# One tile for each result bank in the second half, and a new written order of work

## The chip, the core and the metric

The kernel runs on one core of a Trainium2 chip. The core has five engines that work side by side, each in the order of its own queue: TensorE (PE: matmuls, which write PSUM), VectorE (DVE) and ScalarE (ACT), which read PSUM and SBUF, GpSimd (POOL), which reaches SBUF alone, and SyncE (SP), which here issues every DMA. They wait for one another by semaphores. The time is the device time of one execution in microseconds, the median of several.

## What is computed

Attention through a few packed queries, then two MoE layers of one expert each, all on 4608 tokens (8 batches of 576) of 512 features:

```python
p_packed = softmax(0.125 * p @ k.T) @ v        # 8 batches x 8 heads, 32 packed rows, head size 64
x   = softmax(0.125 * q @ p_packed.T) @ p_packed       # -> [4608, 512]

h   = x @ w_in                                 # first MoE, 512 -> 2048
P   = a0 + a1*h + a2*h**2 + a3*h**3
Q   = 1 + |b0|*|h| + |b1|*h**2
x2  = (P / (Q + 1e-6)) @ w_out                 # 2048 -> 512

h   = x2 @ v_in                                # second MoE
out = (h - tanh(h)) @ v_out
```

The weights come as 64-bit floats and are taken apart on the chip. Each product is made of three fp32r matmuls: both factors are split into a high and a low part, and low x low is left out.

## The kernel before

**A plan, and its order.** Every piece of work (a group of matmuls, one elementwise step, one DMA) is given to a `Plan` by `add`, with its engine (or two engines to choose from), a cost, what it needs, a due time, and what it must stand behind. `Plan.run` gives the pieces out one by one; each engine's instructions stand in its queue in that order, and a tile framework adds the semaphores, by the tiles that each instruction reads and writes. The list `ORDER` names pieces in the order in which they are to be given; a `+` says that the second of two engines takes the piece (DVE, where the choice is POOL or DVE). When the list is at its end, or its next piece isn't ready, the plan chooses by its costs, the due times (`DUE`) and a tolerance for each engine (`SLACK`). In the kernel before, the list has 3021 pieces and ends in the middle of the superblock s = 1 of the second MoE; the plan chose the last 944.

**First half** (to about 766 us). For a block of tokens n (10 of 384 or 512) and a pair p of weight slices (8), g = 8n + p. `l1` makes h of the first MoE, 2 x (384 or 512) columns, in one PSUM tile of two banks. ACT reads it in `ft` and `fu` (lines 878 and 882), DVE in `f2` and `f3` (893 and 897); `fw`, `fq` (890) and `r` make the reciprocal of Q, `b0` to `b3` (910 to 919) the quotient's high and low part, and `l2h` and `l2l` multiply them by `w_out` into the four accumulators of `ps_acc`. `fq` and `b3`, like the steps `ss`, `sn`, `sl` of the softmax and the low parts `w2` of the weights, are done by POOL or DVE. Weight pieces are loaded by `raw.j.c` into two buffers and unpacked (`d1`, `dA`, `d`, `wh`, `w2`). The attention of a half batch u runs through `sc`, `mx`, `ex`, `et`, `ta`, `av`, `y`, `bt`, `bd`; `k`, `v`, `q`, `w1`, `w1d` and `st` are DMAs, and `g` folds the packed values into the weights (`gH`, `gL`).

**Second half.** The first 1536 tokens of the second MoE go by plain products: `l3` makes h for one slice f of 128 features (16 slices, three blocks b of 512 tokens, 12 matmuls each, line 988), `th` takes the tanh (ACT, line 1003), `su` (for b > 0 the steps g11 to g22) subtracts (DVE, line 1007). Meanwhile DVE, ACT and POOL make the sums of weights that Strassen's scheme needs (`ps`, `pm`, `ph`, `pl`), and `pb`, `pd` store them. Then come superblocks s of 1024 tokens by a Strassen-Winograd scheme with seven products: `m3(s, j, i)` is product i (in the order 1, 6, 7, 5, 2, 4, 3, six matmuls each, line 1205) of the feature block j = 0 to 7, for s = 1 to 3, and `m4(s, i, f)` the second layer, for s = 0 to 3. A j of `m3` has four result banks: a (products 1, 2), b (6), c (7, 4), d (5, 3). ACT copies a (`p1`, line 1214); DVE makes `u2` = b + p1 (1216), `u3` = c + u2 (1218), `h22` = d + u3 (1220), then `h21` = c + u2 and `h12` = d + u2 (1222, 1224).

**PSUM.** There are eight banks. Four are `ps_acc`, one tile each (acc). The other four are the pool `ps_h`: two tiles of two banks each, taken in turn by `ring` (tile name h) by everything else: `sc`, `et`, `av`, `g`, `sm`, `l1`, pairs of `l3`, and in `m3` and `m4`. In `m3` an even j takes both h tiles (a, b in one, c, d in the other), an odd j the four acc tiles. The tile framework lets a tile's writer and its readers on different engines wait for one another.

Of the kernel before, what the change touches and what calls it, by code (L numbers as in the profile page):

```python
# [35 lines left out]
l2l.1 f2.3 l1.4 fq.3 w1d.1 z.3 f3.3 dA.10 d1.10 w1d.3 ft.4 d.10 l2h.2 fu.4 g.0.6 f2.4 raw.11.0 b3.2 wh.10.0 wh.10.1
f3.4 gH.0.6 av.3 r.3 gL.0.6 w2.6+ raw.11.1 k.4 y.3 fw.4 w2.7+ w1.1.0 d1.11 l2l.2 b0.3 bt.3 l1.5 raw.12.0 raw.12.1
dA.11 bd.3 b1.3 fq.4+ ft.5 fu.5 b2.3 w1d.4 d.11 r.4 f2.5 sc.4 mx.4 raw.13.0 f3.5 b3.3 dA.12 d1.12+ ex.4 l2h.3 d.12
fw.5 sm.1 et.4 raw.13.1 wh.12.0 fq.5 ta.4 si.1 z.4 wh.12.1 l1.6 sx.1 w1d.5 w2.8+ d1.13 dA.13 ft.6 w2.9+ l2l.3 k.5 b0.4
v.4 fu.6 raw.14.0 d.13 ss.1 sc.5 f2.6 raw.14.1 mx.5 f3.6 r.5 ex.5 l2h.4 av.4 b1.4 se.1 v.5 b0.5 wh.13.1 d1.14 et.5 y.4  # L40
wh.13.0 bt.4 bd.4 sz.1 dA.14 w1d.7 g.1.0 k.6 b2.4 ta.5 w2.11+ gH.1.0 b3.4+ sn.1+ w2.10 p.3 fw.6 gL.1.0 l2l.4 gH.1.1
z.5 raw.15.0 av.5 y.5 gL.1.1 bt.5 d.14 fq.6 bd.5 so.1 g.0.7 gH.0.7 sc.6 gL.0.7 sh.1 r.6 raw.15.1 l1.7 l2h.5 ft.7 mx.6
b1.5 fu.7 sl.1+ b2.5 ex.6 wh.14.0 d1.15 b3.5 dA.15 f2.7 f3.7 w2.12+ fw.7 z.6 b0.6 d.15 et.6 wh.14.1 b1.6 l1.8 w1d.6
wh.15.0 w2.13+ l2l.5 ta.6 ft.8 v.6 w1.1.2 av.6 fq.7+ fu.8 wh.15.1 w2.14 y.6 k.7 l2h.6 r.7 w2.15 f2.8 rx f3.8 bt.6 l1.9
bd.6 g.1.2 b2.6 fw.8 b0.7 b3.6+ ft.9 l2l.6 l2h.7 fq.8+ w1.1.4 fu.9 b1.7 b2.7 gH.1.2 b3.7 gL.1.2 gH.1.3 f2.9 f3.9 l2l.7
fw.9 gL.1.3 r.8 l1.10 sp.0.0 fq.9 l1.11 sp.0.1 b0.8 r.9 b1.8 st.0.0 ft.10 b2.8 b0.9 fu.10 b3.8 l2h.8 st.0.1 f2.10
f3.10 fw.10 ft.11 b1.9 f2.11 fq.10+ g.1.4 p.4 gH.1.5 b2.9 l2h.9 fu.11 q.2 gH.1.4 f3.11 gL.1.4 gL.1.5 sm.2 fw.11 w1.1.6
l2l.8 sc.7 fq.11 si.2 r.10 l1.12 sx.2 r.11 b3.9 mx.7 b0.10 l2l.9 ex.7 b1.10 ft.12 b0.11 fu.12 ss.2+ et.7 f2.12 f3.12
z.7 fw.12 v.7 ta.7 l2h.10 av.7 fq.12 l1.13 b2.10 b1.11 se.2 sz.2 y.7 b3.10+ r.12 bt.7 ft.13 b2.11 bd.7 fu.13 f2.13
f3.13 l2h.11 sn.2 k.8 g.1.6 gH.1.6 gL.1.6 l2l.10 l1.14 gH.1.7 b3.11 gL.1.7 fw.13 fq.13+ l2l.11 r.13 fu.14 b0.12 fw.14  # L50
l1.15 b1.12 b0.13 b2.12 fq.14+ ft.14 b3.12 l2h.12 fu.15 ft.15 w1.2.0 p.5 so.2 f2.14 l2l.12 f3.14 g.2.0 fw.15 gH.2.1
f2.15 b1.13 b2.13 sh.2 l2h.13 gH.2.0 r.14 fq.15+ w1.2.2 f3.15 gL.2.0 sl.2 gL.2.1 b0.14 b1.14 sc.8 mx.8 l1.16 r.15
b2.14 ft.16 b0.15 b3.13 l2h.14 f2.16 ex.8 fu.16 l1.17 l2l.13 fw.16 f3.16 b3.14+ g.2.2 b1.15 fq.16+ ft.17 b2.15 fu.17
l2l.14 f2.17 l2h.15 gH.2.2 gL.2.2 f3.17 gH.2.3 l1.18 fw.17 fq.17+ b3.15+ r.16 gL.2.3 b0.16 r.17 b1.16 ft.18 fu.18
l2l.15 sp.1.0 sp.1.1 b0.17 l1.19 w1.2.4 b1.17 l2h.16 b2.16 fw.18 b2.17 f2.18 fq.18 f3.18 g.2.4 ft.19 st.1.1 fu.19
l2h.17 f2.19 st.1.0 f3.19 r.18 gH.2.4 b3.16 gL.2.4 q.3 gH.2.5 b0.18 fw.19 fq.19+ l1.20 b1.18 gL.2.5 l2l.16 ft.20
w1.2.6 fu.20 b2.18 sm.3 r.19 f2.20 si.3 b3.17 b3.18 f3.20 sx.3 fw.20 l2h.18 l1.21 fq.20+ b0.19 g.2.6 r.20 w1.3.0 b1.19
ft.21 l2l.17 b2.19 l2h.19 ss.3+ fu.21 b0.20 b3.19+ gH.2.7 f2.21 l2h.20 gH.2.6 gL.2.6 fw.21 fq.21 f3.21 b1.20 se.3
l2l.18 r.21 l1.22 fu.22 ft.22 l2l.19 v.8 b2.20 gL.2.7 b0.21 fw.22 b3.20+ b1.21 b2.21 sz.3 fq.22+ f2.22 z.8 l1.23 f3.22
ft.23 sn.3 l2h.21 fu.23 r.22 g.3.0 so.3 w1.3.2 f2.23 fw.23 l2l.20 f3.23 gH.3.1 b3.21 gH.3.0 et.8 l2l.21 sh.3 ta.8  # L60
fq.23 gL.3.0 gL.3.1 av.8 sl.3+ l1.24 y.8 bt.8 r.23 b0.22 b1.22 ft.24 bd.8 fu.24 b2.22 b0.23 l2h.22 l1.25 fw.24 f2.24
b3.22+ ft.25 f3.24 fq.24+ g.3.2 b1.23 b2.23 b3.23 f2.25 fu.25 w1.3.4 l2h.23 gH.3.2 f3.25 fw.25 gL.3.2 gH.3.3 fq.25+
k.9 r.24 l1.26 r.25 ft.26 gL.3.3 l2l.22 fu.26 b0.24 b1.24 b2.24 l2l.23 b0.25 fw.26 v.9 sp.2.0 l1.27 f2.26 st.2.0 fq.26
f3.26 sp.2.1 b1.25 ft.27 b3.24 st.2.1 f2.27 g.3.4 gH.3.4 gL.3.4 fu.27 f3.27 l2h.24 r.26 l1.28 gH.3.5 b2.25 b0.26
gL.3.5 fw.27 sc.9 ft.28 fq.27+ q.4 b1.26 mx.9 fu.28 ex.9 f2.28 l2h.25 b2.26 f3.28 z.9 b3.25+ w1.3.6 r.27 b0.27 b1.27
fw.28 fq.28+ l2l.24 et.9 ta.9 sm.4 si.4 r.28 l2l.25 l1.29 l2h.26 sx.4 ft.29 b3.26 fu.29 ss.4+ av.9 l2l.26 f2.29 f3.29
b0.28 y.9 g.3.6 fw.29 b2.27 fq.29+ bt.9 se.4 gH.3.7 bd.9 gH.3.6 sz.4 gL.3.6 sn.4+ k.10 l2h.27 gL.3.7 b1.28 p.6 r.29
sc.10 mx.10 ex.10 w1.4.0 l1.30 ft.30 b3.27+ b2.28 fu.30 l1.31 b0.29 so.4 l2h.28 fw.30 b1.29 sh.4 f2.30 z.10 l2l.27
ft.31 f3.30 fq.30 fu.31 f2.31 g.4.0 r.30 f3.31 et.10 b3.28 gH.4.0 gH.4.1 l2h.29 sl.4+ b2.29 gL.4.0 gL.4.1 fw.31 fq.31+
ta.10 v.10 av.10 r.31 l1.32 b0.30 b1.30 b2.30 b3.29+ y.10 bt.10 bd.10 fu.32 l2l.28 l1.33 l2l.29 b0.31 fw.32 ft.32  # L70
fq.32+ f2.32 l2h.30 r.32 f3.32 ft.33 b3.30+ f2.33 fu.33 b1.31 l2l.30 k.11 b2.31 b3.31+ fw.33 w1.4.2 f3.33 fq.33+ r.33
b0.32 l1.34 g.4.2 b1.32 l2h.31 b2.32 l2l.31 ft.34 gH.4.3 gH.4.2 f2.34 gL.4.2 fu.34 f3.34 fw.34 sp.3.0 gL.4.3 w1.4.4
sp.3.1 l1.35 fq.34 b3.32+ fu.35 b0.33 g.4.4 b1.33 b2.33 ft.35 gH.4.4 l2h.32 gL.4.4 gH.4.5 f2.35 l2h.33 fw.35 st.3.1
r.34 gL.4.5 fq.35 f3.35 r.35 l1.36 b0.34 b1.34 ft.36 b0.35 b3.33+ sc.11 b1.35 fu.36 l2h.34 st.3.0 f2.36 f3.36 fw.36
# [1851 lines left out]
```

## Time and profile before

| | |
|---|---|
| median of 3 runs | 1509.12 us (1508.44 to 1509.66) |
| profiled execution | 1511.86 us, span of its instructions 1509.7 us |
| PE busy / DVE / ACT / POOL | 1449.2 / 1249.9 / 891.0 / 268.8 us |
| PE clock granted, mean | 0.988 of full speed |
| moved by DMA | 257.86 MB |
| chain that ended last | PE 79% of the span, DVE 11%, ACT 5% |

A busy time is the union of an engine's instructions. Matmuls overlap in their records and their ends are modelled, so two matmuls 0.23 us apart stand there with 0.39 us each, and a gap of PE looks shorter than it is; the distance between starts is the sounder measure. In a timeline, instructions of one line and form that follow each other closely are one row with a count; the bracket says how long the engine was idle before it, and who ended that.

### The profile page before, as it was taken

Reading aid. Unit: us, or ns where it says so; the run is one execution under the profiler, and the core shown is the slowest. Engines: PE = TensorE matmul, PEld = TensorE weight load, DVE = VectorE, ACT = ScalarE, POOL = GpSimd, SP = SyncE. Lnnn points to the kernel's source line nnn. Section 1 sums busy time; section 2 is a strip of 40 time slices with the busy share of each in tenths; the row PEclk is TensorE's granted clock in tenths of the full one; section 3 lists DMA queues with packets and bytes.
Section 4 is the critical chain, followed back from the end, with each engine's and each line's share of the span. In section 5 each row is a group of like instructions: output and inputs, shape, how many; then the busy total and the mean of one; then the engine's idle time right before and its main releaser. Section 6 shows DMA issues by size and latency. Waiting matters only on the chain.

```text
span 1509.7 us, 21786 instructions
## 1 busy us (share of the span) xinstructions
PE 1449.2 (96%) x8448; PEld 1192.3 (79%) x8448; DVE 1249.9 (83%) x1590; ACT 891.0 (59%) x1232; POOL 268.8 (18%) x167
## 2 busy tenths in 40 slices
...
GB/s 305 240 261 179 91 56 128 88 129 57 177 56 87 137 56 112 56 115 60 64 163 180 258 237 265 270 285 235 205 194 278 229 181 213 232 213 195 209 199 136
DMA packets 74998, 257.86 MB, mean 171 GB/s; under 512 B 7184, under 2 KB 25744, under 8 KB 60048
## 3 DMA queue, kind: packets, MB, share of 16 engines
...
q8 instruction: 67, 1.10, 0.3%
q14 instruction: 35, 0.29, 0.1%
...
## 4 chain that ended last, share of the span: by engine, by line
PE 79%; DVE 11%; ACT 5%; issue 2%; DMA 1%; POOL 1%; SPq 0%; DVEq 0%; ACTq 0%; POOLq 0%
PE acc L868 20%; PE acc L1205 19%; PE h L1205 15%; PE h L855 11%; PE h L988 8%; PE h L721 2%; DVE t L893 1%; DVE t L897 1%; PE acc L1028 1%; PE acc L1029 1%; PE acc L1030 1%; ACT u L882 1%; DVE gh L910 1%; DMA raw<-in_w_dram 1%; DVE m L912 1%
## 5 line engine op out<-in xcount | busy, mean ns | idle before, releaser
L855 PE MATMUL h<-ah,slot 128*128 128x320 f32 (+3 forms) x1024 | 215.1, 304 | 0.0
L868 PE MATMUL acc<-gh,slot 128*128 128x512 f32 (+1 forms) x800 | 171.8, 366 | 0.0
L855 PEld LDWEIGHTS h<-ah,slot 128*128 128x128 f32 x1024 | 170.7, 193 | 1.1
L868 PE MATMUL acc<-raw,slot 128*128 128x512 f32 (+1 forms) x720 | 165.4, 380 | 0.7 <-DVE raw L910 0.7
L868 PEld LDWEIGHTS acc<-gh,slot 128*128 128x128 f32 x800 | 143.5, 188 | 25.9 <-issue 8.9
L855 PE MATMUL h<-al,slot 128*128 128x192 f32 (+3 forms) x512 | 151.0, 308 | 9.8 <-DVE t L897 5.1
L868 PEld LDWEIGHTS acc<-raw,slot 128*128 128x128 f32 x720 | 130.3, 188 | 33.0 <-issue 8.7
L1244 ACT ACTIVATE yh<-slot 128x512 fp32r<-128x512 f32 x140 | 87.7, 631 | 73.6 <-DVE yl L1248 25.5
L855 PEld LDWEIGHTS h<-al,slot 128*128 128x128 f32 x512 | 98.4, 192 | 19.5 <-issue 7.7
L1248 DVE TENSOR_TENSOR yl<-slot,yh 128x512 fp32r<-128x512 f32 x140 | 98.3, 714 | 17.8 <-ACT yh L1244 17.3
L878 ACT ACTIVATE t<-h,coa 128x1024 f32<-128x1024 f32 (+1 forms) x80 | 89.2, 1117 | 39.1 <-PE h L855 39.0
L893 DVE TENSOR_TENSOR t<-t,h 128x1024 f32<-128x1024 f32 (+1 forms) x80 | 88.5, 1110 | 26.7 <-ACT u L882 26.1
L882 ACT ACTIVATE u<-h 128x1024 f32<-128x1024 f32 (+1 forms) x80 | 74.8, 935 | 46.5 <-PE h L855 13.8
L897 DVE SCALAR_TENSOR_TENSOR t<-t,coa,h 128x1024 f32<-128x1024 f32 (+1 forms) x80 | 93.6, 1171 | 6.0 <-ACT u L882 4.4
L868 PE MATMUL acc<-gl,slot 128*128 128x384 f32 (+1 forms) x400 | 93.9, 378 | 2.6 <-POOL gl L919 1.3
L988 PE MATMUL h<-xh,slot 128*128 128x512 f32 x256 | 84.0, 402 | 3.6 <-DVE slot L1007 2.8
L868 PEld LDWEIGHTS acc<-gl,slot 128*128 128x128 f32 x400 | 73.9, 195 | 16.2 <-issue 3.1
L1205 PE MATMUL h<-slot,rg 128*128 128x512 f32 x336 | 80.8, 393 | 5.3 <-DVE slot L1220 2.3
L1244 ACT ACTIVATE yh<-ex 128x512 fp32r<-128x512 f32 x84 | 53.1, 632 | 51.3 <-PE acc L1205 16.9
L1205 PEld LDWEIGHTS h<-slot,rg 128*128 128x128 f32 x336 | 62.2, 188 | 22.6 <-DVE slot L1220 5.2
L1205 PE MATMUL acc<-yh,raw 128*128 128x512 f32 x256 | 78.9, 389 | 0.0
L1205 PE MATMUL acc<-yh,rg 128*128 128x512 f32 x256 | 78.8, 389 | 0.0
...
## 6 DMA issues: line engine op xcount, KB each, us to landing
...
```

Of the source, the lines that this page charges most:

```text
L721: pe.matmul(out=ps[32 * hp:32 * hp + 32, i, :], lhsT=pp[b][r, hp, :], rhs=x[r, hp, :])
L855: pe.matmul(out=ps[:, f, t], lhsT=x, rhs=y, start=(i == 0), stop=(i == len(seq) - 1))
L868: pe.matmul(out=acc_t[n][m][:, 0:XW[n]], lhsT=w2_slot[2 * p + f][:, o:o + 128], rhs=x[:, f, :], start=(p == 0 and part == 512 and f == 0), ...
L878: act.activation(out=t_t[g], in_=hv(g), func=AF.Identity, scale=a3, bias=a2)
L882: act.activation(out=u_t[g], in_=hv(g), func=AF.Abs)
L893: dve.tensor_tensor(out=t_t[g], in0=t_t[g], in1=hv(g), op=ALU.mult)
L897: dve.scalar_tensor_tensor(out=t, in0=t, scalar=a1, in1=hv(g), op0=ALU.add, op1=ALU.mult)
L910: dve.scalar_tensor_tensor(out=gh_t[g], in0=t, scalar=a0, in1=r, op0=ALU.add, op1=ALU.mult)
L988: pe.matmul(out=hy(b, f), lhsT=a, rhs=w, start=(j == 0), stop=(j == len(seq) - 1))
L1205: pe.matmul(out=to, lhsT=a, rhs=b, start=(first and n == 0 and i in (1, 6, 7, 5)), stop=(last and n == len(seq) - 1), skip_group_check=True,)
L1244: act.activation(out=yh_t[s, i, f], in_=g_of(GSRC[i], f), func=AF.Copy)
L1248: by.tensor_tensor(out=yl_t[s, i, f], in0=g_of(GSRC[i], f), in1=yh_t[s, i, f].bitcast(F32), op=ALU.subtract)
```

## The change

1. `ps_h` is closed after the first half (`open banks`, ordered behind the last `f3`), and its four banks come back as four tiles of one bank each. `pair` hands them out two by two, in the turn that `ring` would have had next. `l3`, `m3` and `m4` use `pair`.
2. The plan learns that readers of one PSUM tile on different engines come one after the other: `add` takes `on`, `run` remembers when each engine has last read that tile, and `apart` puts a start behind the other engines' reads. It is given for `gH`, `gL`, `ft`, `fu`, `f2`, `f3`.
3. The plan's latency of a load goes from 3.0 to 4.0 us for `k`, `v`, `q`, `p`, `w1`, `w1d`, `id` and the first 16 `raw`; `DUE` and `SLACK` have new numbers.
4. Three pieces get an order among themselves: `xr` of the first block behind its first, `th.3` behind `th.2`, `l3.0` behind the new `open b` in place of the last `l1`.
5. `ORDER` is new from the first line on, and names all 3965 pieces.

```diff
-SLACK = {"ALT": 0, "DVE": 0.0, "PE": 468.9, "ACT": 81.3, "POOL": 0.0, "SP": 0.0}
+SLACK = {"ALT": 0, "DVE": 7.5, "PE": 525.8, "ACT": 0, "POOL": 0, "SP": 734.4}
...
 ORDER = """
...
-wh.6.1 fw.1 w2.3+ q.1 fq.1+ dA.7 l1.2 gL.0.4 d1.7 b2.0 d.7 b3.0 av.2 ft.2 fu.2 y.2 raw.8.0 f2.2 raw.8.1 bt.2 f3.2
-g.0.5 r.1 b0.1 bd.2 d1.8+ raw.9.0 dA.8 v.3 l2l.0 raw.9.1 fw.2 d.8 gH.0.5 fq.2+ wh.8.1 wh.8.0 gL.0.5 sc.3 mx.3 w2.5
...
+d1.6+ dA.6 ft.1 b0.0 d.6 v.2 gH.0.3 gL.0.3 wh.6.1 l2h.0 av.2 w2.3+ fu.1 f2.1 wh.6.0 raw.7.1 w2.2 fw.1 f3.1 y.2 dA.7
+b1.0 fq.1+ k.3 p.2 g.0.4 gH.0.4 b2.0 b3.0 bt.2 bd.2 w1d.2 w1d.3 raw.8.0 gL.0.4 sc.3 l1.2 d1.7 mx.3 r.1 ex.3 raw.8.1
+d.7 ft.2 b0.1 fu.2 w1.1.0 b1.1 d1.8+ dA.8 d.8 fw.2 f2.2 et.3 l2l.0 fq.2 raw.9.0 ta.3 f3.2 wh.8.0 l2h.1 w2.4+ raw.9.1
...
+        seen = {}
+
+        def apart(engine, x):
+
+            return max([t for e, t in seen.get(x[10], {}).items() if e != engine], default=0)
...
-            return t
+            return max(t, apart(engine, x)) if x[10] else t
...
+            if x[10]:
+                seen.setdefault(x[10], {})[engine] = end[name]
...
-    ps_h = pool_of(ctx, "ps_h", bufs=2, space=PSUM)
+    sh = ctx.enter_context(ExitStack())
+    ps_h = pool_of(sh, "ps_h", bufs=2, space=PSUM)
+    banks_p, uses = [], []
...
     def ring(key):
+        uses.append(key)
         ps_t[key] = ps_h.tile([128, 2, 512], F32, tag="h", name="h")
         return ps_t[key]
+
+    def open_banks():
+        sh.close()
+        banks_p.append(pool_of(ctx, "ps_b", space=PSUM))
+
+    def pair(key):
+        i = len(uses) % 2
+        uses.append(key)
+        ps_t[key] = [banks_p[0].tile([128, 512], F32, tag=f"b{i}{x}", name=f"b{i}{x}") for x in range(2)]
+        return ps_t[key]
...
     def hy(b, f):
-        return ps_t[f // 2, "y", b][:, f % 2, :]
+        return ps_t[f // 2, "y", b][f % 2]
...
-                t = ring(("m3", s, j, 0))
-                bank["a"], bank["b"] = t[:, 0, :], t[:, 1, :]
+                bank["a"], bank["b"] = pair(("m3", s, j, 0))
...
-            t = ring(("m4", s, i))
+            t = pair(("m4", s, i))
...
+    add(("open b",), None, 0, open_banks, [], 0, behind=[("f3", total - 1)])
...
-            kw["behind"] = [("l1", total - 1)]
+            kw["behind"] = [("open b",)]
```

## Rows read from the trace of the kernel before

**Rows 1.** The page, busy time, share of the span and instructions of each engine.

```profile
PE 1449.2 (96%) x8448; PEld 1192.3 (79%) x8448; DVE 1249.9 (83%) x1590; ACT 891.0 (59%) x1232; POOL 268.8 (18%) x167
```

**Rows 2.** Stretches: length; busy PE, PEld, DVE, ACT, POOL; clock; DMA share; GB/s.

```profile
0.00:50.00 50.00, 25.13 (x255) 15.47 (x255) 26.38 (x42) 25.59 (x42) 1.85 (x8) 0.84 0.80 272
50.00:100.00 50.00, 41.36 (x367) 33.62 (x366) 46.13 (x58) 46.36 (x64) 12.13 (x8) 0.92 0.85 287
100.00:150.00 50.00, 46.24 (x437) 39.09 (x438) 43.56 (x53) 42.35 (x62) 15.87 (x9) 0.97 0.51 176
150.00:766.00 616.00, 606.87 (x4211) 509.09 (x4210) 572.29 (x585) 439.91 (x522) 156.64 (x74) 1.00 0.25 93
766.00:1037.00 271.00, 266.72 (x1166) 218.00 (x1165) 219.32 (x319) 140.85 (x218) 54.57 (x49) 0.99 0.70 242
1037.00:1114.00 77.00, 72.31 (x312) 57.55 (x311) 40.36 (x61) 23.40 (x42) 23.73 (x19) 1.00 0.60 206
```

**Rows 3.** Timeline of PE, s = 1: start, length, instruction, count, idle before.

```profile
1037.35 8.32 PE L1205 MATMUL h<-slot,rg 128*128 128x512 f32 x36
1047.95 9.70 PE L1205 MATMUL acc<-slot,raw 128*128 128x512 f32 x42
1057.49 1.52 PE L1205 MATMUL h<-slot,rg 128*128 128x512 f32 x6
...
1068.91 9.68 PE L1205 MATMUL acc<-slot,raw 128*128 128x512 f32 x42
1078.43 8.32 PE L1205 MATMUL h<-slot,rg 128*128 128x512 f32 x36
...
1098.57 1.52 PE L1205 MATMUL h<-slot,rg 128*128 128x512 f32 x6
...
1110.81 4.47 PE L1205 MATMUL acc<-slot,raw 128*128 128x512 f32 x19
```

**Rows 4.** Timeline of PE, s = 2 and s = 3.

```profile
1216.34 10.13 PE L1205 MATMUL h<-slot,raw 128*128 128x512 f32 x42
1226.31 9.68 PE L1205 MATMUL acc<-slot,rg 128*128 128x512 f32 x42
...
1410.20 10.14 PE L1205 MATMUL h<-slot,rg 128*128 128x512 f32 x42
1420.18 9.68 PE L1205 MATMUL acc<-slot,raw 128*128 128x512 f32 x42
```

**Rows 5.** Timeline of DVE, s = 2: `u3` on h, on acc.

```profile
1202.44 0.69 DVE L1218 TENSOR_TENSOR u<-h,u 128x512 f32<-128x512 f32 x1 [1.40 <-PE h L1205]
...
1211.55 0.69 DVE L1218 TENSOR_TENSOR u<-acc,u 128x512 f32<-128x512 f32 x1
```

**Rows 6.** Waits of PE from 766 to 1037 us: total, times, longest.

```profile
PE h L988 <- DVE slot L1007: 2.8, 2, 1.9
PE h L988 <- ACT t L1003: 1.4, 2, 0.7
```

**Rows 7.** Line 988 (`l3`): ns min/median/max, first and last start in us.

```profile
L988 PE MATMUL h<-xh,slot x256: 388/395/628, 767.0 to 960.9; 128*128 128x512 f32 x128
...
L988 PEldq EVENT_SEMAPHORE  x2: 51/51/51, 765.6 to 776.0; - x2
```

**Rows 8.** Groups of `fq` before 150 us: count, busy us, mean ns, idle before.

```profile
L890 POOL TENSOR_TENSOR m<-u,r 128x768 f32<-128x768 f32 x3 | 5.5, 1842 | 14.8 <-ACT r L886 8.3 <-DVE raw L567 4.7 <-ACT y L698 1.8
...
L890 DVE TENSOR_TENSOR m<-u,r 128x768 f32<-128x768 f32 x5 | 4.8, 952 | 0.0
```

**Rows 9.** Timeline of POOL and DVE around 639 us.

```profile
638.91 2.39 POOL L919 TENSOR_TENSOR gl<-m,r 128x1024 fp32r<-128x1024 f32 x1 [2.90 <-DVE m L890]
...
639.28 3.11 DVE L910 SCALAR_TENSOR_TENSOR raw<-t,coa,raw 128x1024 fp32r<-128x1024 f32 x1
```

**Rows 10.** Stretches of 10 us (columns as in the second group).

```profile
30.00:40.00 10.00, 4.94 (x63) 1.76 (x56) 9.04 (x16) 8.05 (x15) 1.48 (x1) 0.53 0.89 297
40.00:50.00 10.00, 7.58 (x28) 6.66 (x26) 6.60 (x9) 6.46 (x9) 0.00 (x0) 0.67 0.48 171
```

More of the change, by code (lines that the diff above doesn't have):

```diff
@@ L36 @@
[L36 to L74, printed above, removed]
-mx.11 l1.37 v.11 ex.11 b2.34 q.5 fq.36+ ft.37 l2l.32 b2.35 et.11 fu.37 w1.4.6 l2l.33 f2.37 f3.37 b3.34 ta.11 r.36
@@ new lines @@
+wh.8.1 w2.5+ l1.3 z.3 q.1 g.0.5 r.2 d1.9 b2.1 b0.2 ft.3 fu.3 dA.9 b3.1+ fw.3 raw.10.0 b1.2 f2.3 gH.0.5 d.9 f3.3
+raw.10.1 fq.3 l2l.1 gL.0.5 d1.10 b2.2 l1.4 b3.2+ v.3 av.3 dA.10 k.4 d.10 raw.11.0 fu.4 ft.4 f2.4 y.3 wh.10.1 wh.10.0
+l2h.2 fw.4 bt.3 bd.3 f3.4 w2.7+ r.3 w2.6+ sc.4 raw.11.1 sm.1 dA.11 mx.4 p.3 w1d.5 si.1 l2l.2 fq.4 ex.4 b0.3 raw.12.0
+d1.11 b1.3 r.4 d.11 b2.3 et.4 l1.5 ta.4 fu.5 raw.12.1 k.5 ft.5 dA.12 b3.3 z.4 sx.1 f2.5 g.0.6 v.4 f3.5 gH.0.6 d1.12
+ss.1 l2h.3 raw.13.0 gL.0.6 b0.4 fw.5 raw.13.1 d.12 sc.5 se.1 av.4 y.4 bt.4 w1d.7 wh.12.0 bd.4 mx.5 ex.5 l2l.3 wh.12.1
@@ new lines @@
+w2.8+ et.5 w1d.6 v.5 b1.4 fq.5+ l1.6 dA.13 w2.9+ sz.1 d1.13 ta.5 fu.6 b2.4 g.1.0 ft.6 gH.1.0 d.13 f2.6 gH.1.1 wh.13.0
+wh.13.1 raw.14.0 gL.1.0 r.5 f3.6 z.5 b3.4 l2h.4 fw.6 g.0.7 gL.1.1 gH.0.7 av.5 w2.11 raw.14.1 w2.10+ sn.1+ fq.6 gL.0.7
+so.1 y.5 dA.14 d1.14 bt.5 b0.5 d.14 k.6 l2l.4 w1d.4 v.6 bd.5 sh.1 b1.5 r.6 b2.5 sl.1 sc.6 l1.7 fu.7 ft.7 l2h.5 mx.6
+wh.14.0 f2.7 f3.7 raw.15.0 raw.15.1 ex.6 b3.5+ w2.12+ et.6 d1.15 wh.14.1 l1.8 b0.6 dA.15 d.15 w1.1.2 w2.13+ fw.7 ta.6
+ft.8 z.6 l2l.5 av.6 wh.15.0 wh.15.1 p.4 l2h.6 f2.8 fq.7 fu.8 y.6 w2.15+ w2.14 r.7 rx f3.8 b1.6 bt.6 fw.8 b0.7 b2.6
@@ new lines @@
+l2l.61 g.7.2 b1.63 f3.65 fw.65 gH.7.3 fq.65 gH.7.2 gL.7.2 r.65 l2h.63 gL.7.3 b2.63 b3.63 w1.7.4 r.64 l1.66 b0.65 fu.66
+fw.66 b0.64 b1.64 l2l.62 ft.66 b2.64 f2.66 l2l.63 b3.64 sp.7.0 sp.7.1 l1.67 l2h.64 f3.66 ft.67 fq.66+ fu.67 b1.65
+fw.67 g.7.4 l2l.64 st.7.0 st.7.1 gH.7.5 gH.7.4 l2h.65 b2.65 fq.67+ b3.65+ gL.7.4 f2.67 r.67 l2l.65 r.66 raw.16.0 q.9
+f3.67 w1.7.6 gL.7.5 b0.66 b1.66 b0.67 raw.16.1 l1.68 sm.9 b2.66 b1.67 fu.68 si.9 ft.68 b3.66 sx.9 f2.68 f3.68 fw.68
+ss.9 fq.68+ l2h.66 b2.67 l2l.66 b3.67+ d1.16 l1.69 se.9 r.68 sz.9 l2h.67 sn.9 fu.69 g.7.6 ft.69 fw.69 f2.69 dA.16
@@ new lines @@
+f3.69 so.9 gH.7.6 gL.7.6 fq.69 b0.68 b1.68 l2l.67 sh.9 gH.7.7 gL.7.7 r.69 l1.70 d.16 ft.70 fu.70 b2.68 b3.68 l2h.68
+fw.70 l1.71 f2.70 f3.70 b0.69 b1.69 fq.70+ raw.17.0 sl.9+ b2.69 l2l.68 l2h.69 b3.69 wh.16.1 fu.71 ft.71 raw.17.1 r.70
+l1.72 f2.71 open_x f3.71 fw.71 b0.70 fq.71+ l2l.69 b1.70 fu.72 l2h.70 ft.72 b2.70 l1.73 w3.1+ r.71 b3.70+ l2l.70
+xr.0.0 xr.0.1 b0.71 b1.71 fw.72 fq.72+ b2.71 d1.17 l2h.71 wh.16.0 ft.73 fu.73 f2.72 xh.0.1 r.72 b3.71 xh.0.0 f3.72
+w3.0 dA.17 fw.73 raw.18.0 l2l.71 f2.73 f3.73 l1.74 b0.72 fq.73+ sp.8.0 b1.72 sp.8.1 d.17 b2.72 xl.0.1+ r.73 b3.72+
@@ new lines @@
+l2h.72 ft.74 l1.75 b0.73 raw.18.1 fu.74 fw.74 b1.73 ft.75 fq.74+ b2.73 f2.74 st.8.1 f3.74 l2l.72 b3.73 l2h.73 xl.0.0+
+l1.76 fu.75 r.74 b0.74 fw.75 l2l.73 f2.75 f3.75 fq.75 b1.74 ft.76 l2h.74 st.8.0 xr.0.2 r.75 fu.76 l1.77 b2.74 b3.74+
+xr.0.3 b0.75 b1.75 fw.76 d1.18 fq.76+ dA.18 l2l.74 r.76 fu.77 l2h.75 xh.0.2 b2.75 b3.75 f2.76 l2l.75 fw.77 f3.76 d.18
+b0.76 wh.17.1 wh.17.0 l1.78 ft.77 wh.18.1 wh.18.0 fq.77+ w3.2+ w4.0+ xl.0.2 raw.19.0 raw.19.1 r.77 l2h.76 f2.77 f3.77
+w4.1+ ft.78 xh.0.3 w3.3+ b1.76 l1.79 fu.78 b0.77 b2.76 b3.76 ft.79 dA.19 l2h.77 f2.78 raw.20.0 xl.0.3 f3.78 d1.19
@@ new lines @@
+l2l.76 f2.79 b1.77 raw.20.1 fw.78 d.19 fq.78+ b2.77 d1.20 wh.19.0 wh.19.1 w3.4+ w4.2+ fu.79 b3.77+ dA.20 r.78 f3.79
+raw.21.0 open_b d.20 fw.79 fq.79+ l3.0.0 b0.78 l3.0.1 wh.20.0 wh.20.1 th.1 r.79 w4.3+ w3.5+ b1.78 th.0 l2l.77 l3.0.2
+raw.21.1 l2h.78 su.1 b2.78 d1.21 dA.21 th.2 raw.22.0 l3.0.3 b0.79 su.0 d.21 wh.21.1 b3.78+ wh.21.0 th.3 raw.22.1 w3.6+
+w4.4+ raw.23.0 dA.22 b1.79 d1.22 b2.79 raw.23.1 d.22 l3.0.4 wh.22.1 l2l.78 wh.22.0 l2h.79 b3.79+ w3.7+ l2l.79 dA.23
+w4.5+ sp.9.0 d1.23+ su.2 raw.24.0 l3.0.5 sp.9.1 su.3 raw.24.1 st.9.1 l3.0.6 st.9.0 open_y th.5 yh.0 d.23 yl.0 l3.0.7
@@ L232, in __init__, with add @@
         self.rings, self.work, self.aliases = dict(rings), {}, {}
-    def add(self, name, engine, cost, run, after=(), due=0.0, take=None, free=(), behind=(), late=None, port=None):
+    def add(self, name, engine, cost, run, after=(), due=0.0, take=None, free=(), behind=(), late=None, port=None, on=None):
         assert name not in self.work, name
         port = "POOL" in engine if port is None and engine else port
-        self.work[name] = [engine, cost, run, list(after), due, take, list(free), list(behind), late, port]
+        self.work[name] = [engine, cost, run, list(after), due, take, list(free), list(behind), late, port, on]
     @contextmanager
```

388 lines of the change are left out of this document (235 added, 153 removed).

## The prediction

> **What bounds the kernel now.** I read the busy line of the page first, then stretches of the run by engine, then what TensorE (PE) waited for in each stretch, and last the timeline of PE and VectorE (DVE) around those waits. PE is busy 1449.2 us of the span [rows 1], so the most that any order of work could give back is some 60 us. The stretches [rows 2] tell where those lie: 24.9 us in the first 50 (loads, before and around the first matmuls), 8.6 and 3.8 in the next two 50s, 9.1 in the 616 us of the first MoE, 4.3 in the stretch of `l3`, 4.7 in the first Strassen superblock (s = 1); what is left, some 5, comes after it. From 50 to 150 us DVE and ScalarE (ACT) are as busy as PE or busier (46 of 50), and the DMA engines are at 0.85; from 150 to 766 DVE is at 93% beside a PE at 98.5%. So the first half has three near-full engines and little to win by order alone. From 766 on PE alone is full, and each of its gaps is time lost.
>
> A busy PE row has modelled ends, so the gaps are best taken from start to start. In s = 1 the j's of `m3` (42 matmuls each) alternate: the even j's write the ring tiles (h), the odd ones the four `ps_acc` tiles. The first two odd j's last 9.54 and 9.52 us, the even ones 10.60, 11.42 and, the last, 12.24; the third even j and its odd neighbour last 20.14 together, as the first two do, so that one is 10.60 again [rows 3]. In s = 2 and 3 the row of an even j is 10.13 us long, that of an odd one 9.68 [rows 4], where the first unbroken pair and the last stand for eight even j's alike. Nothing differs between them but the tile: an h tile is one tile of two banks. [rows 5] shows what that does: on h, step `u3` (reads bank c) starts 1.40 us late, released by PE, which was still writing the other bank of that tile; on acc, `u3` follows its predecessor directly and runs beside PE's writes to another bank.
>
> **The change, part by part.**
>
> *Banks of m3.* The pairs become two tiles each, so that an even j has the odd j's situation. s = 1: 10.60 + 11.42 + 10.60 + 12.24 - 4 x 9.53 = 6.7 us. s = 2 and 3: 8 x 0.45 = 3.6 us. Together 10.3 us, all on PE's path, because PE does nothing else in that time. The ends: 10.3, if every even j becomes an odd one; 3.6, if the extra 0.6 to 2.3 us of the s = 1 ones belong to DVE's order of work there and come back. DVE is only 40.4 of 77 us busy in that stretch [rows 2], so I take 10.3. What is late next is DVE's own queue: `h22` stands behind `u3`, and `m3` of i = 3 waits for it, with a slack of two groups of six matmuls.
>
> *Banks of l3.* PE waits 2.8 us for DVE and 1.4 for ACT in this stretch [rows 6], in four pieces, where `th` and `su` of a pair ran late and PE came back to the tile. With single banks the next `l3` needs only the `su` of its own bank. But here DVE is 219 of 271 us busy [rows 2] with the making of Strassen weights, whose order is new too. Ends: 4.2 gained, or 2 lost if the new order puts more of that work ahead of a `su`; I take half, 2.1.
>
> *More tiles, more waits.* 24 pairs of `l3`, 24 of `m3` and 8 of `m4` may each need one wait more on PE's sequencer, at 51 ns [rows 7]: 56 x 0.051 = 2.9 us at most. They lie ahead of matmuls that are queued already, so I take nothing; if that cover goes, it is the 2.9.
>
> *open b, and the `behind` of l3.0, xr and th.3.* The old pool closes when `f3` of the last group has been given, so `l3.0` is ordered behind it. PE has `l2h`, `l2l` work of the last groups in both orders at that point, and both orders put two `l3` there before it ends. Nothing; at worst PE waits for one more piece of DVE, about 1 us [rows 8].
>
> *on, apart, DUE, SLACK, late.* They change what the planner believes, not what an instruction does. The new ORDER names all 3965 pieces of work (the old one 3021; the last 944 were picked by costs and due times), so these numbers pick nothing. Zero.
>
> *ORDER before 766 us.* Instructions are the same; engines of some change. Counting the marks in both orders over the first MoE, GpSimd (POOL) gets 7 more `fq` and 2 more `ss`, and 3 `b3`, 2 `sl`, 2 `w2` and 1 `sn` less: one piece more of some 86. In the opening, POOL has six `fq` instead of four up to `b3.8`. Such an `fq` takes 1.84 us there and 0.95 on DVE [rows 8], so two chains to `l2h` grow by 0.9. On SP's queue the last weight piece of the first MoE (`raw.15.1`) stands behind 1.1 MB more than before, `raw.11.1` behind 1.6 MB (the load `w1.1.0` and the stores `w1d` come earlier); `raw.7.1` stands behind 0.65 MB less. At 287 GB/s [rows 2] that is 3.9 and 5.7 us later, 2.3 earlier. Against that, `av.2` and `bt.2`, which stood back to back and left PE waiting for ACT, now have `g.0.4` between them. Signs on both sides: zero, with ends of 10.8 gained (half of the 8.6 + 3.8 + 9.1 us of idle PE) and 7.5 lost (5.7 + 2 x 0.9).
>
> A POOL piece is not free for DVE: while POOL ran a `b3` of 2.39 us, a DVE instruction that began 0.37 us after it took 3.11 and ended 1.09 us after it: some 2.0 us of standing [rows 9]. The Trainium skill ("SBUF — State Buffer", section "Who interferes with whom") says that a VectorE instruction with two SBUF inputs is shut out for the whole of a GpSimd instruction that reads SBUF. By that rule each of the seven moved `fq` could cost DVE 2.0 us of standing where it saves one piece of 0.95, up to 7 us in all; by the count of pieces above, one more on POOL in 86, it is 1.
>
> The sum: 10.3 + 2.1 = 12.4 us. The profiled execution took 1511.86 us (span 1509.7 and 2.2 around it), 2.7 above the median of the runs shown, 1509.12. So 1499.5 beside the profiled execution, 1496.7 beside the median: I forecast **1496.7**.
>
> **The rivals.**
>
> *The opening pays it back (slower).* Place: 60 to 120 us. The loads of `raw.11` to `raw.15` come 5.7 us later, the two `fq` chains add 1.8, and PE stands for those 7.5 us. Between 30 and 50 us PE was busy 12.5 of 20 us and its granted clock was 0.53 and 0.67 [rows 10]; such a spell at a mean of 0.60, between the two levels of 1.2 and 2.4 GHz, loses another 8. Together 15.5: 1509.1 - 12.4 + 15.5 = 1512.2. It decides from the point at which the second half starts 12.4 us later. For it: three full engines leave no room to catch up. Against: the raw loads are paced by two buffers that DVE sets free, not by the DMA alone, whose share falls to 0.51 after 100 us.
>
> *The opening and the first MoE gain as well.* The plan now knows that `ft`, `fu`, `f2`, `f3` can't read h side by side, and places DVE's work accordingly. Half the idle of PE from 50 to 766 us goes: 1496.7 - 10.8 = 1485.9. Against: DVE has 93% of that stretch, so what is filled in one place is missing in another.
>
> *Only the small waits go.* The s = 1 and `l3` waits are DVE's queue, and the new order queues it as badly; 3.6 us remain: 1505.5.
>
> *It does not do what it says.* The tile tracker already keeps banks apart, and the even j's are late for another reason; 1509. [rows 5] speaks against it.
>
> **How the numbers follow.** 0.2% is 3 us, about what can be told from no change. Forecast (1490 to 1503): 0.45. Gain in the first half too: 0.15. Only the small waits: 0.17, about half of it within 3 us of before. Opening pays back: 0.17. No effect: 0.06. So faster 0.69, same 0.14, slower 0.17. The range 1484 to 1511 leaves out little at the bottom, most of the slower case at the top.
>
> **What would show it.** Even and odd j's of `m3` of 9.5 us alike, in all of s = 1 to 3: the first term right. `u3` on the new banks starting without a wait for PE: the mechanism right. No wait of `l3` above 0.7 us: the second term. The start of the first `l3` (767.0 before [rows 7]) tells the first half apart: within 3 us of that it was zero; after 775 the opening paid back; before 760 it gained. Even j's still at 10 us or more, or `l3` starting over 10 us later, make the prediction wrong.

## The result, and the profile after

The changed kernel takes **1484.01 us** (median of 4 runs, 1483.25 to 1485.63), the kernel before 1508.78: a ratio of 0.984, 95% interval 0.9823 to 0.9857. It is 24.8 us faster, twice the 12.4 forecast. A second set of 4 runs gave 1484.32 (0.9839, 0.9822 to 0.9856).

The two profiled executions have spans of 1509.72 and 1482.17 us. Cut at the first matmul of each stage, the 27.55 us between them come from here (some 3 of them lie in the execution: the profiled one of the kernel before took 1511.86 us, that much above its median):

| stretch | before | after | difference |
|---|---|---|---|
| start to `l1` of group 11 | 144.57 | 139.97 | -4.60 |
| from there to `l1` of group 79 | 616.21 | 603.09 | -13.12 |
| from there to the first `m4` | 200.40 | 201.95 | +1.55 |
| `m3`, s = 1 | 82.99 | 76.16 | -6.83 |
| `m3`, s = 2 and 3 | 156.01 | 152.33 | -3.68 |
| the four `m4`, and the end | 309.54 | 308.67 | -0.87 |

So there are two gains (17.7 in the first half, 10.5 in `m3`) and a loss between them. The changed kernel's page, and its stretches (columns as in [rows 2]):

```profile
PE 1436.9 (97%) x8448; PEld 1191.6 (80%) x8448; DVE 1237.0 (83%) x1588; ACT 897.5 (61%) x1235; POOL 280.5 (19%) x168
```

```profile
0.00:50.00 50.00, 25.57 (x257) 15.69 (x258) 27.75 (x42) 26.22 (x42) 2.20 (x8) 0.80 0.88 289
50.00:100.00 50.00, 42.28 (x426) 34.52 (x425) 46.20 (x60) 46.07 (x68) 12.41 (x7) 0.93 0.83 285
100.00:150.00 50.00, 47.70 (x412) 39.60 (x414) 47.38 (x56) 45.39 (x63) 14.82 (x8) 1.00 0.49 165
150.00:740.00 590.00, 590.00 (x4132) 496.38 (x4129) 556.00 (x570) 432.00 (x508) 155.04 (x71) 1.00 0.27 95
750.00:757.00 7.00, 0.56 (x5) 0.27 (x3) 7.00 (x9) 6.96 (x10) 0.09 (x1) 0.72 0.11 37
757.00:760.00 3.00, 3.00 (x7) 2.42 (x8) 3.00 (x4) 2.71 (x4) 0.00 (x0) 0.51 0.72 268
760.00:765.00 5.00, 5.00 (x24) 4.20 (x24) 2.02 (x4) 1.42 (x3) 0.00 (x0) 1.00 0.58 201
757.00:1021.00 264.00, 264.00 (x1159) 218.01 (x1160) 208.56 (x322) 137.09 (x211) 43.28 (x35) 0.99 0.72 242
1021.00:1098.00 77.00, 77.00 (x341) 63.75 (x341) 48.61 (x77) 26.63 (x47) 16.92 (x14) 1.00 0.62 220
```

Against [rows 2]: from 150 to 740 us PE has no idle time left in the records, and none in `l3` or `m3`. The kernel before had in the same 590 us:

```profile
150.00:740.00 590.00, 581.60 (x4066) 484.15 (x4065) 546.50 (x556) 417.78 (x495) 149.10 (x70) 1.00 0.26 95
```

One stall is new, from 750 to 757 us: PE busy 0.56 of 7 us, DVE and ACT full.

**`m3`.** PE's timeline of s = 1 after, the answer to [rows 3]:

```profile
1021.26 9.68 PE L1296 MATMUL b<-slot,rg 128*128 128x512 f32 x42
1030.79 9.68 PE L1296 MATMUL acc<-slot,raw 128*128 128x512 f32 x42
...
1078.38 9.68 PE L1296 MATMUL b<-slot,rg 128*128 128x512 f32 x42
1087.90 9.68 PE L1296 MATMUL acc<-slot,raw 128*128 128x512 f32 x42
```

Even j's (on the new banks, b) and odd ones (acc) are 9.52 us alike. `u3` on either kind, the answer to [rows 5], with 0.6 us in both places, where h had 1.40 and acc none:

```profile
1177.88 0.69 DVE L1309 TENSOR_TENSOR u<-b,u 128x512 f32<-128x512 f32 x1 [0.61 <-PE b L1296]
...
1187.40 0.69 DVE L1309 TENSOR_TENSOR u<-acc,u 128x512 f32<-128x512 f32 x1 [0.60 <-PE acc L1296]
```

**The stall.** PE's waits after 745 us (the answer to [rows 6]), and its timeline there:

```profile
PE b L1081 <- DVE t L990: 6.4, 1, 6.4
PE acc L961 <- DVE gh L1003: 0.6, 1, 0.6
```

```profile
745.93 3.08 PE L961 MATMUL acc<-gh,slot 128*128 128x384 f32 x16 [0.62 <-DVE gh L1003]
748.89 1.66 PE L961 MATMUL acc<-gl,slot 128*128 128x384 f32 x8
756.99 0.76 PE L1081 MATMUL b<-xh,slot 128*128 128x512 f32 x1 [6.44 <-DVE t L990]
757.55 0.63 PE L1081 MATMUL b<-xl,slot 128*128 128x512 f32 x1
757.98 0.63 PE L1081 MATMUL b<-xh,slot 128*128 128x512 f32 x1
```

The first `l3` waits for `f3` (line 990) of group 79, the last of all, which DVE begins only here:

```profile
755.84 1.00 DVE L990 SCALAR_TENSOR_TENSOR t<-t,coa,h 128x768 f32<-128x768 f32 x1
```

So the first pair must share banks with the last `l1`, although `pair` was meant to go on in `ring`'s turn. Which banks these are is told by the program's addresses and by no profile: the last `l1` has its h tile in banks 4 and 5, and the first pair gets banks 4 and 5 again, since the reopened pool gives out banks in the order in which its tiles are first made, whatever `pair` counts. The other two banks, which `f3` of group 78 had set free at 748.72, lay idle. Experiment 3 puts this to the test.

**The first half.** What PE waited for from 150 us on, before (up to 766, the four longest of nine), then after (up to 750, all there is):

```profile
PE h L855 <- DVE t L897: 3.7, 4, 1.9
PE acc L868 <- POOL gl L919: 1.3, 2, 0.7
PE h L721 <- PE h L855: 0.9, 1, 0.9
PE h L721 <- PE h L644: 0.8, 1, 0.8
```

```profile
PE acc L961 <- DVE gh L1003: 0.6, 1, 0.6
```

And what DVE waited for at `f2` and `f3` (lines 893 and 897; 986 and 990 after) from 0 us on, before and after:

```profile
DVE t L893 <- ACT u L882: 26.1, 21, 3.1
...
DVE t L897 <- ACT u L882: 4.4, 6, 1.1
```

```profile
DVE t L986 <- ACT t L971: 10.2, 13, 2.0
DVE t L986 <- ACT u L975: 4.5, 7, 1.4
```

Before, `f2` stood 26.1 us for `fu`, though it needs nothing that `fu` makes: both read one h tile, and the semaphores let the readers through one by one. The Trainium skill ("PSUM — Partial Sum Buffer", section "PSUM bank collisions raise a hardware error") says why readers are kept apart: two engines may not touch one bank in the same cycle, two readers included, so accesses are to be guarded bank by bank. The 26.1 us of waits agree as to readers, but they are those of the framework's semaphores; no run here shows what an unguarded access would do. The two-bank h tile guards more than that rule asks.

### The profile page after: what moved, and what is told of

It is laid out like the page before. It is cut to its first block, busy times and chain, and to the rows that moved or that the text cites. A ratio compares the mean times of both kernels' runs of the same rounds, so it can differ in the third digit from the quotient of the medians.

```text
span 1482.2 us, 21855 instructions
## 1 busy us (share of the span) xinstructions
PE 1436.9 (97%) x8448; PEld 1191.6 (80%) x8448; DVE 1237.0 (83%) x1588; ACT 897.5 (61%) x1235; POOL 280.5 (19%) x168
## 4 chain that ended last, share of the span: by engine, by line
PE 90%; DVE 4%; ACT 3%; issue 1%; DMA 1%; SPq 0%; DVEq 0%; ACTq 0%
PE acc L961 24%; PE acc L1296 19%; PE b L1296 17%; PE h L948 13%; PE b L1081 9%; PE h L801 3%; PE acc L1121 1%; PE acc L1122 1%; PE acc L1123 1%; PE h L724 1%; PE h L769 1%; DMA raw<-in_w_dram 1%; DVE t L986 1%; PE h L754 1%; DVE m L1009 0%
## 5 line engine op out<-in xcount | busy, mean ns | idle before, releaser
L961 PEld LDWEIGHTS acc<-gh,slot 128*128 128x128 f32 x800 | 143.5, 188 | 30.7 <-issue 10.7
L986 DVE TENSOR_TENSOR t<-t,h 128x1024 f32<-128x1024 f32 (+1 forms) x80 | 88.5, 1108 | 15.2 <-ACT t L971 10.2
L983 POOL TENSOR_TENSOR m<-u,r 128x1024 f32<-128x1024 f32 (+1 forms) x27 | 58.4, 2162 | 166.3 <-DVE t L986 46.6
L1081 PE MATMUL b<-xh,slot 128*128 128x512 f32 x256 | 83.3, 399 | 6.4 <-DVE t L990 6.4
L1296 PE MATMUL b<-slot,rg 128*128 128x512 f32 x336 | 77.5, 389 | 0.0
```

The costliest lines, as they stand in the source:

```text
L961: pe.matmul(out=acc_t[n][m][:, 0:XW[n]], lhsT=w2_slot[2 * p + f][:, o:o + 128], rhs=x[:, f, :], start=(p == 0 and part == 512 and f == 0), ...
L983: by.tensor_tensor(out=q_m[g], in0=u_t.pop(g), in1=r_t[g], op=ALU.mult)
L986: dve.tensor_tensor(out=t_t[g], in0=t_t[g], in1=hv(g), op=ALU.mult)
L1081: pe.matmul(out=hy(b, f), lhsT=a, rhs=w, start=(j == 0), stop=(j == len(seq) - 1))
L1296: pe.matmul(out=to, lhsT=a, rhs=b, start=(first and n == 0 and i in (1, 6, 7, 5)), stop=(last and n == len(seq) - 1), skip_group_check=True,)
```

## The experiments

Line numbers differ from kernel to kernel; `l1`, `l3` and so on are named in the text. Intervals are 95% intervals of the ratio to the kernel before, which took 1508.1 to 1508.9 us beside these runs.

**1. The banks alone.** The old order on the new tiles.

```diff
 ORDER: as before, its last 944 pieces written out as the plan chose them
-... l3.0.0 l3.0.1 ... f3.79 ...
+... f3.79 open_b l3.0.0 l3.0.1 ...
```

> The order of work, DUE, SLACK and the load latency of the kernel before, written out to the last piece, with the change's single-bank tiles for l3, m3 and m4; only l3.0.0 and l3.0.1 stand behind f3.79, where the pool closes. Theory (the tiles give the second half, the order the first): the even j's of m3 fall to 9.5 us, some 10.5 us gained there as in the changed kernel (82.99 to 76.16 us in s = 1, 1.8 in s = 2 and 3 each); the first l3 starts within 5 us of 767, late by the wait for the last f3; l3 gains the 4 us of PE's waits. So 1495 to 1500 us, and what the order is worth is the other 11 to 16. Rival (the tiles are worth only the 3.6 us of the regular even j's, the rest is the order's): m3 of s = 1 stays above 80 us, l3 at 194, 1505 us.

Measured: **1496.9 us** (0.9922, 0.9909 to 0.9936). `m3` takes 76.16 us in s = 1, 2 and 3, as in the changed kernel: 10.5 us from the tiles alone. From `l1` of group 79 to the first `m4` it takes 198.64 us (200.40 before): all that PE waits for there is at the place where the two `l3` were moved away, in PE's timeline:

```profile
762.16 2.94 PE L888 MATMUL acc<-gh,slot 128*128 128x384 f32 x16
769.12 4.61 PE L888 MATMUL acc<-gh,slot 128*128 128x384 f32 x16 [4.02 <-DVE gh L930]
773.57 1.57 PE L888 MATMUL acc<-gl,slot 128*128 128x384 f32 x8
774.98 0.39 PE L1008 MATMUL b<-xh,slot 128*128 128x512 f32 x1
```

The theory holds for `m3` and for the total. The stretch of `l3` gained 1.8 us, not the 4 expected, and the first `l3` came at 774.98, 8 us late instead of 5.

**2. The order alone.** The new order on the old tiles.

```diff
-                bank["a"], bank["b"] = pair(("m3", s, j, 0))
+                t = ring(("m3", s, j, 0))
+                bank["a"], bank["b"] = t[:, 0, :], t[:, 1, :]
```
(and so for c and d, `l3` and `m4`; no pool is closed)

> The changed kernel's whole order of work, with the old tiles of two banks kept for l3, m3 and m4 (no pool is closed). Theory (tiles second half, order first half): the first l3 starts at 749 to 752 us, since PE no longer stands 6.4 us there for the last f3; m3 goes back to 78 us in s = 2 and 3 and to 78 or more in s = 1 (7 to 10.5 us lost in all); l3 loses 2 to 6. So 1487 to 1493 us. Rival (the order would have repaired the second half without new tiles): m3 of s = 1 at 76 to 77 us, and the whole at 1481 or less.

Measured: **1519.43 us** (1.0064, 1.0047 to 1.0081): slower than the kernel before, and outside both expectations. The first half is that of the changed kernel (`l1` of group 79 at 743.05), the first `l3` starts at 750.37. Then that gain is lost and more: 11.1 us more than in the changed kernel up to the first `m4`, 1.8 in that, and in `m3` 12.95, 6.92 and 1.91. PE's waits in `m3`, s = 1, and the first j's:

```profile
PE h L1297 <- DVE u L1310: 4.1, 2, 2.0
PE h L1297 <- DVE slot L1312: 1.6, 3, 0.8
PE h L1297 <- ACT p L1306: 1.4, 2, 0.7
```

```profile
1034.18 6.96 PE L1297 MATMUL h<-slot,rg 128*128 128x512 f32 x30
1043.17 1.72 PE L1297 MATMUL h<-slot,rg 128*128 128x512 f32 x6 [2.04 <-DVE u L1310]
1045.68 2.93 PE L1297 MATMUL h<-slot,rg 128*128 128x512 f32 x6 [0.78 <-DVE slot L1312]
1048.41 11.13 PE L1297 MATMUL acc<-slot,raw 128*128 128x512 f32 x42
```

PE waits for `u3` (line 1310) to have read one bank of h before it may write the other. On pairs the new order is worse than the old one (`m3` of s = 1 takes 89.11 us, 82.99 before); on single banks both give 76.16. Banks alone -12, order alone +10.6, both -24.8: the parts don't add.

**3. The other turn of the pairs.**

```diff
     def open_banks():
         sh.close()
         banks_p.append(pool_of(ctx, "ps_b", space=PSUM))
+        for x in range(2):
+            banks_p[0].tile([128, 512], F32, tag=f"b0{x}", name=f"b0{x}")
...
-        i = len(uses) % 2
+        i = (len(uses) + 1) % 2
```

> The changed kernel, with its pairs of single banks handed out in the other turn and made in that order when the pool opens: the first l3 then writes the two banks that the last but one l1 had, which f3.78 sets free, not those of the last l1, which f3.79 sets free. Theory (the 6.4 us in which PE stands before the first l3 come from that turn alone): the gap goes, the first l3 starts 5 to 6.5 us earlier, and all after it moves along: 1477.5 to 1479.5 us. Rival (the gap is work of DVE that PE needs soon in any case, and only moves to the next l3 or l2 pieces): under 2 us gained, 1482 to 1484.

Measured: **1480.43 us** (1478.22 to 1480.87; 0.9807, 0.9794 to 0.982), 3.6 to 3.9 less than the two medians of the changed kernel, and the fastest of all. In PE's timeline the first `l3` (line 1083) now follows without a gap:

```profile
747.25 3.07 PE L963 MATMUL acc<-gh,slot 128*128 128x384 f32 x16 [0.63 <-DVE gh L1005]
750.21 1.68 PE L963 MATMUL acc<-gl,slot 128*128 128x384 f32 x8
751.73 0.39 PE L1083 MATMUL b<-xh,slot 128*128 128x512 f32 x1
```

It starts 5.4 us ahead of the last `f3`, which it had to wait for before:

```profile
757.15 1.00 DVE L992 SCALAR_TENSOR_TENSOR t<-t,coa,h 128x768 f32<-128x768 f32 x1
```

From `l1` of group 79 to the first `m4` it takes 197.63 us, 4.3 less than the changed kernel, not 6.4: 1.8 us of new waits for DVE's `su` steps come in behind it, among others. The theory holds as to the cause; the size lies between it and the rival.

**4. The engines exchanged, both ways.** 82 pieces of the first half (33 `fq`, 29 `b3`, 20 others) are done by another engine in the changed order. First the new order with the old engines, then the old order (on the new banks) with the new engines.

```diff
-... fq.0 ... b3.2+ ...
+... fq.0+ ... b3.2 ...
```

> The changed kernel, its order untouched, but 82 pieces (fq, b3, ss, sn, sl, w2, d1) of the first half go back to the engine that did them in the kernel before; GpSimd gets 7 fq less, 3 b3, 2 sl and 2 w2 more. Theory A (the first half gained by the sequence in which DVE and ACT take their pieces, so that f2 waits less for fu): little is lost, within 5 us of 1484, though the pieces were not placed for these engines. Theory B (it gained by which engine does what: DVE, the fullest beside PE, was relieved): 8 to 16 us lost, 1492 to 1500 us, PE again standing for f3 at l1.

> The banks alone (order of the kernel before, 1496.9 us), with the engines that the changed kernel gives to the 82 pieces fq, b3, ss, sn, sl, w2, d1 of the first half. Theory (an order and its engines fit only each other, as the 34 us lost by the opposite exchange say): 10 us or more slower than the banks alone, over 1507. Rival (these engines relieve DVE and carry the gain of the first half): 1480 to 1490 us.

Measured: **1518.05 us** (1.0064, 1.005 to 1.0079), 34 us lost, and **1542.16 us** (1.0226, 1.0209 to 1.0243), 45 us lost against the banks alone. In the first, theory A is refuted and B's size too small; in the second the theory holds. PE waits for `f3` at `l1` again, from 100 and from 150 us on:

```profile
PE h L875 <- DVE t L917: 7.8, 8, 3.2
```

```profile
PE h L875 <- DVE t L917: 10.2, 6, 3.0
```

These waits are only a part of the 34 and 45 us; where the rest lies is not shown. An order and its choice of engines fit only each other. How much of the 17.7 us either has by itself can't be told from these two.

**5. Openings exchanged.** The old opening (403 pieces, to `l1` of group 11) with the new rest, then the new opening (412 pieces) with the old rest; both on the new banks.

```diff
-ORDER = new[:412] + new[412:]
+ORDER = old[:403] + [pieces of new that are left]
```

> The changed kernel, but its first 403 pieces are those of the kernel before, in that order and on those engines (to l1 of group 11); from there on the pieces that are left come in the changed order. Group 11 starts at 144.6 us in the kernel before, at 140.0 in the changed one. Theory (the opening is worth those 4.6 us, the other 13 of the first half are gained between 150 and 740 us, where PE stops waiting): 1487 to 1491 us. Rival 1 (the first MoE is DVE's, so a late opening is caught up or a good one runs out): 1482 to 1486. Rival 2 (the order after 150 us only fits its own opening): over 1495.

> The other way round: the first 412 pieces (to l1 of group 11) as in the changed kernel, the rest in the order and on the engines of the kernel before, with the banks (alone they took 1496.9 us). Theory (each stretch keeps what it has: the changed opening is worth 2.5 to 4.6 us, the rest of the first MoE the other 12): l1 of group 79 at 754 to 757 us instead of 758.7, PE again waiting for f3 between 150 and 740 us, 1492 to 1495 us. Rival (the changed opening only helps because of what follows it): 1496 us or more.

Measured: **1482.35 us** (0.982, 0.9802 to 0.9838), which fits rival 1 by its time, but not by its trace. `l1` of group 11 starts at 142.61, 2.6 us after that of the changed kernel, and of group 79 at 745.90, 2.8 after: nothing is caught up. It is won back because the 7.3 us to the first `l3` hold no stall: it starts at 753.20, and the last `f3` only at 758.66. By the program's addresses the exchange shifted the h tiles by one turn: the last `l1` lies in banks 6 and 7, and the first `l3` finds 4 and 5 free, as in experiment 3. A delay at group 11 arrives whole at group 79 (in experiment 3 too: 1.3 us at both), and PE has next to no idle time between them: from 140 us on PE is the bound under the new order.

The other: **1499.46 us** (0.9939, 0.9925 to 0.9954); the rival holds. Group 11 starts at 138.50, 4.7 before that of the banks alone, group 15 at 185.35 and group 79 at 758.76 (banks alone 184.91 and 758.70). Two idle times of PE, of 1.50 and 2.09 us, take up most of it within 20 us; the rows name no releaser for them. So under the old order something other than PE sets the pace there, and a better opening is worth nothing.

**6. `f2` moved out of `fu`'s way.** In 12 groups, on the banks alone.

```diff
-... fu.7 sl.1+ b2.5 ... f2.7 f3.7 w2.12+ ...
+... fu.7 sl.1+ b2.5 ... w2.12+ f2.7 f3.7 ...
```

> The banks alone (order of the kernel before, 1496.9 us), with one thing moved: in 12 groups of the first MoE in which f2 stood at the head of DVE's queue waiting for ACT's fu on the same h tile (15.6 us of idle DVE in all), the next other DVE piece of the list goes ahead of f2 (and of f3 where it stood between). Theory (what the plan now knows of readers of one tile is what the first half gained by): the idle DVE is filled, l1 of group 79 starts 5 to 10 us sooner than 758.7, 1487 to 1492 us. Rival (f3 comes later in these groups, and PE waits for it at l1 instead, or the idle DVE is off the path): 1494 to 1502 us.

Measured: **1502.75 us** (0.9957, 0.994 to 0.9973), 5.9 slower than the banks alone; slower as the rival says, and just past its 1502. (The profiled execution, 1505.59, was the slowest of five.) DVE's wait of `f2` for `fu` fell from 17.9 to 10.7 us between 150 and 766 us, and `l1` of group 79 came 8.4 us later. In the trace PE stands twice at `l1` (groups 8 and 20) for an `f3` that the edit had put off; `z`, named in the first row, is the piece right behind that `f3`:

```profile
124.88 0.33 PE L875 MATMUL h<-al,slot 128*128 128x192 f32 x1 [2.64 <-DVE z L674]
241.55 0.48 PE L875 MATMUL h<-al,slot 128*128 128x256 f32 x1 [2.14 <-DVE t L917]
```

Both times the piece that went ahead was not ready itself, and DVE stood for it in place of `f2`:

```profile
121.96 0.86 DVE L1466 TENSOR_TENSOR slot<-raw,slot 128x512 fp32r<-128x512 f32 x1 [1.68 <-ACT slot L1462]
238.27 0.69 DVE L740 TENSOR_TENSOR slot<-h,slot 128x512 fp32r<-128x512 f32 x1 [3.89 <-ACT slot L736]
```

So the idle time was not filled but moved: between group 11 and group 79 DVE does 571.8 us of work in 615.5 on the banks alone, and 571.7 in 618.7 here. In these two places PE pays for a later `f3`; what a real filling of DVE's wait would be worth is not shown.

**7. The plan left to itself.** The new list is cut after `l1` of group 11; with what the plan knows of readers, and without.

```diff
-            return max(t, apart(engine, x)) if x[10] else t
+            return t
```

> The changed kernel with its list cut after l1 of group 11 (412 pieces): the plan chooses the other 3553 by its costs, DUE, SLACK and what it knows of the readers of one tile. All theories: slower than the changed kernel by more than 10 us, since the list was the better order; l1 of group 79 after 755 us. It is there to be set beside the next one.

> As the one before, but the plan no longer puts a reader behind the other engine's reader of the same tile (apart gives nothing). Theory (that knowledge is what keeps DVE from standing at f2): DVE waits 10 us or more longer for ACT's fu at f2, and l1 of group 79 starts 5 to 20 us later than with it. Rival (the knowledge changes the order, not the time): the two within 4 us of each other at that point.

Measured: **1522.32 us** with (1.009, 1.0069 to 1.0111), **1542.1 us** without (1.0222, 1.0203 to 1.024). `l1` of group 79 starts at 768.82 and 785.92, so the knowledge is worth 17.1 us where the plan chooses with these costs and due times (others were not tried, and they may have been set for a plan that has it). It isn't worth it by the way expected: `f2`'s wait for `fu` is not among DVE's longer waits in either. PE's waits for `f3` differ, first with, then without:

```profile
PE h L713 <- DVE t L755: 9.1, 5, 3.3
```

```profile
PE h L713 <- DVE t L755: 13.6, 8, 3.4
```

That is 4.5 of the 17.1; waits for `b0` (0.9 against 4.0 us) and `b3` (1.8 against 3.9) grow too. GpSimd's part differs as well, 46 instructions and 101.2 us after 150 us with, 38 and 82.9 without; that this is the cause isn't shown. The written list beats the better of the two by 38 us.

The changed kernel again, beside experiments 4 (second) to 6:

> The changed kernel once more, for the comparison with the others of this group on one chip: 1483 to 1486 us by every theory; its first l3 at 757 us, PE standing 6.4 us before it.

Measured: 1484.32 us, the first `l3` at 757.41, behind 6.42 us of standing PE.

## Why the prediction was right and wrong

- *Banks of m3, 10.3 us: right.* 10.5 in the changed kernel and in the banks alone, all even j's at 9.52 us. The lower end (3.6) rested on DVE's order causing the s = 1 delays; experiment 1 kept that order and they went. The sign "`u3` starts without a wait for PE" was put wrongly: it waits 0.6 us for its own bank, on b as on acc. Experiment 2 shows the mechanism from the other side.
- *Banks of l3, 2.1 us: the sum near, by cancelling.* The banks alone gained 1.8 us up to the first `m4`: PE's waits of [rows 6], 4.2 us, went, and 4.0 us of wait came in where the two `l3` were moved. These two would leave 0.2; but waits cost more than their rows say. Against the usual distances between starts (0.23 us at 512 columns, 0.17 at 384) the kernel before loses some 7 us in this stretch and the banks alone some 5, half speed of TensorE behind the waits included (see the end). In the changed kernel no wait of `l3` itself remained after its first.
- *open b, "nothing; at worst about 1 us": wrong.* It cost 6.4 us of standing, and 1.4 more at half speed. The step failed at "both orders put two `l3` there": it counted the pieces of DVE ahead of `l3`, and not which banks the reopened pool would hand out first. Experiment 3 took back 4.3 us up to the first `m4`.
- *More tiles and waits, nothing: right.* PE has no idle time in `m3` with 24 more pairs of tiles.
- *The new numbers pick nothing: right as far as it goes;* the list names every piece. But experiment 7 shows that what the plan knows is worth 17.1 us when it does choose.
- *ORDER before 766 us, zero: the step that failed.* It gained 17.7 us up to group 79, of which the first `l3` kept 10.0 (767.02 to 756.99), past the mark of 760 that was set for "gained". A part of that can be chance: with the old order group 79 starts at 760.78 and, in experiment 1, at 758.70, with the new one in four executions at 743.05 to 744.37, so the order's gain is 14 to 18 us. The forecast weighed 7 moved `fq` and late loads and found both signs. The 7 are a net count: 82 pieces of the first half changed engine, 33 of them `fq` (20 to GpSimd, 13 away from it), and by experiment 4 these choices go with tens of us. The loads didn't show (group 11 starts 4.6 us early). Its argument that DVE at 93% leaves no room is refuted: DVE did the same work (688.4 us of it to 766 us before, 687.1 to 750 us after) in less time, since 43.7 us of its stretch from 150 to 766 us were idle, far more than PE's 9.1. And 9.1 us was too low for what PE had to give, as it comes from records whose ends are modelled. From group 11 to group 79 PE's idle time went from 9.1 us to none, and its busy rows, of the same matmuls, from 607.1 to 603.1 us: together the 13.1.
- *The total: luck in part.* The time lies at the very end of the range of 1484 to 1511 and outside the forecast's own 1490 to 1503. The rival of a gain in the first half (1485.9, chance 0.15) came within 2 us, but it put that gain at 10.8 and knew of no stall; the 17.7 and the stall happen to leave nearly that. Without the stall (experiment 3) the kernel takes 1480.4. That the plan's knowledge of readers made the gain, as the rival says, isn't shown.
- *Which half the parts belong to* was taken to be separable. It is so from the first half to the second; within each it is not (experiments 2, 4, 5).

Still open: what in the new order removed the 13.1 us between group 11 and group 79. Which waits of PE went is on record for 9.1 of them (for `f3` 3.7, for GpSimd's `b3` 1.3, the others under 1 us each); the other 4.0 are spread over busy rows. The wait of `f2` for `fu` that the change is aimed at fell from 26.1 to 4.5 us (with 10.2 for `ft` in its place), but experiment 6 doesn't decide what that was worth; order and engines could not be taken apart.
